# Window attention and two MLPs: an offset of its own for each group of operations in the planner's order

## The chip, the cores and the metric

One Trainium2 chip, one of its cores. The metric is the device time of one execution in microseconds (us); the kernel before took 952.38 us in the median of 3 runs (952.3 to 956.86).

Engines are named as the profile names them: PE (matrix products), PEld (its loads of weights), DVE, ACT, POOL (GpSimd) and SP (which issues the DMAs).

## What is computed

```python
def _attn_ref(q, k, v):                    # 4 batches, 8 heads, 576 positions, 64 wide
    scores = scale * np.matmul(q, k.transpose(0, 1, 3, 2))
    bias = slopes[:, None, None] * (-np.abs(rel))[None, :, :]
    mask = (rel >= 0) & (rel < 128)
    scores = np.where(mask, scores + bias[None], -1000000000.0)
    ...
    attn = attn / (np.sum(attn, axis=-1, keepdims=True) + 1e-09)
    return np.matmul(attn, v)

x = attention as 2304 tokens x 512
h = x @ w_in;   x = (h * tanh(softplus(h))) @ w_out      # moe:  512 -> 2048 -> 512
h = x @ w_in2;  out = elu(h) @ w_out2                    # moe2: 512 -> 2048 -> 512
```

## The kernel before, in words

**Work.** The tokens go in chunks of 512: chunk `ci` = 0 to 3 holds positions 0 to 511 of one batch, chunk 4 (`B`) the last 64 positions of all four. Attention is done by `unit(b, pr, part)`: one batch, one pair of heads, and queries 0 to 255 (`part` 0), 256 to 511 (1) or 512 to 575 (2). A unit is a chain over all engines: scores (PE, L493 to L503), masks and row minima (DVE, L514, L517), the exponential (ACT, L521), normalisation (L537 to L541: DVE, ACT or POOL), transposition (PE, L562), the mask again (L578 or L587), values (PE, L613), and a copy to SBUF.

**First MLP.** A step `s` of `hidden1` makes one 128x512 tile of hidden values: 12 products of 512 columns or 24 of 256, in pieces of six (L702), then on ACT the Mish function (L709, which needs another activation table than the exponential), a copy `gh` and a difference `gl` (L363) that together carry the value as high and low part. `output1` multiplies both with the second weights into `py` (L730), two steps later in the planner's count. Chunk 0 is done in 16 steps of half the width, so that its first half can start before all its attention is done; steps 16 to 71 are the other chunks. Every product is done three times (high by high, high by low, low by high).

**Weights.** The weights arrive as 64-bit numbers; `load_weights` turns each half of a 128-wide slice (32 for each MLP) into a high and a low part: two instructions on ACT, two on DVE, one on POOL, and then a copy and a difference on whichever engine is free. The 32 of the first MLP run beside attention at the start.

**Second MLP.** `hidden2` (L843), an ELU (L851 to L854, then `gh` and `gl`) and `output2` (L872), 80 steps. The hidden tile is in PSUM, in a ring of two buffers with the tag `h`: a third tile's products wait until the first one's `gl` has been taken.

**Order.** Nothing is emitted in the order of the source. Every operation is recorded in `Plan.op` with the engines that can do it (`ways`), its cost there, what it needs, its buffers and a priority `prio`. `Plan.order` then walks through time: each free engine takes the ready operation of lowest priority whose buffers have room, and where several engines could do it, the one that would finish first. The instructions of each engine stand in that order in the program, and each engine runs its own in order. So a priority decides both the order and the engine. Priorities are made of the step's planned time (`STEP` = 6.96) and offsets in the table `AT`, one for each kind of operation. While PE has nothing to do at the start, `order` puts products into its queue whose result nobody reads (`plan.fill`, L308, "unused"):

```python
if e == "pe" and self.fill and t < self.fill[2] and not self.rings["z"]["next"]:
    out.append(self.fill[1])
```

Of the kernel before, what the change touches and what calls it, by code (L numbers as in the profile page):

```python
# [13 lines left out]
AT = dict(lag=2, step=6.96, late=23.66, copy=1.19, both=0.34, conv=-34.61, conv1=8.2, mish=-3.26, out=-0.67,  # L14
          prep=-6.85, load=-27.75, loadr=12.24, unit=3.02, unit1=3.1, split=6.31, x2=-21.79, w2=1.86, step2=1.49,
          g=-8.44, stage=-21.52, fill=80.0, u0=0.0, u1=5.67, t0=1.26, t1=11.22, t2=4.45, u2=33.61, u3=4.87,
          norma=0.5, normp=8.33, relt=-13.66, d00=-2.11, d01=-2.85, d10=0.27, d11=1.21, dx=3.28, plain=6.14,
          mm2=8.39, first=-1000.0, second=-53.57, wadd=2.54, whi=-10.73, wlo=9.29, norm=-2.13, mask=-3.68, gl=13.52,
          newton=-9.59, elu=-24.7, lead=1, turn=2.71, held=28.54)
# [14 lines left out]
class Buffer:  # L34


    def __init__(self, ring, seq, make):
        self.ring, self.seq, self.make = ring, seq, make
        self.ops, self.real, self.left, self.taken, self.free_at = 0, None, 0, False, None
# [7 lines left out]
class Plan:  # L47
# [6 lines left out]

    WARM = 6.9
# [28 lines left out]
    def op(self, ways, reads=(), writes=(), prio=0.0, moved=0, rows=1.0, table=None, port=False):  # L84
# [20 lines left out]
        self.ops.append(dict(ways=ways, deps=deps, bufs=bufs, prio=prio, moved=moved, rows=rows, table=table, port=port))  # L105

    def order(self):
# [47 lines left out]
        while events:  # L155
# [4 lines left out]
            while again:  # L160
                again = False
                for e, q in waiting.items():
# [63 lines left out]
        return out  # L226

# [13 lines left out]
def mm_cost(n):  # L241
    return 0.000417 * n + 0.0125
# [18 lines left out]
def tile_window_attention_two_mlps(ctx, tc, qkv0, qkv1, qkv2, w1d, w2d, out):  # L261
    nc = tc.nc
# [45 lines left out]
    plan.fill = (256 / 2400 + 0.003, lambda: nc.tensor.matmul(unused[:, :256], ones[:, :P], ones[:, :256], start=True, stop=True), AT["fill"])  # L308
# [10 lines left out]
    def buf(tag, shape, dt=F32, name=None):  # L319
# [4 lines left out]
        def make():  # L324
            t = where.tile([P, words], dt, tag=tag, name=name or tag, bufs=slots)
# [8 lines left out]
        x = plan.buffer(tag, slots, make)  # L334
        return x

# [62 lines left out]
    def load_weights(wd, into, f, k, pr, stage):  # L399

        hi, lo = (buf(nm, (DM,), F32R) for nm in (("wih", "wil"), ("woh", "wol"))[k])
        into[f, k] = hi, lo
        for o in range(0, DM, HW):
# [24 lines left out]
                lambda hi=hi, o=o: hi()[:, o:o + HW], [bits] + [(hi, x) for x in parts], [(lo, x) for x in parts], pr + AT["wlo"])  # L428

# [3 lines left out]
    def unit(b, pr, part, t0, dt, banks, first=None):  # L433
# [8 lines left out]
        tp = t0 + AT["prep"] * dt  # L442
        cut = [sum(W[:i]) for i in range(4)]
# [21 lines left out]
        vn = lambda: vr().rearrange("p (n h d) -> p n h d", h=2, d=D)  # L465
        if not plain:
# [5 lines left out]
            sub(2 * nk, lambda: kk()[D:], lambda: k2()[D:], lambda: kk()[D:], [tiles[1]], [kk], tp)  # L472
        prob = []
# [176 lines left out]
        else:  # L650
            pieces = [(0, scores, 4), (3, turn, 4), (6, values, 0)]
        return [(t0 + o * dt, (lambda fn=fn, i=i, t=t0 + o * dt: fn(i, t))) for o, fn, i in pieces] + [
            (t0 + 8 * dt, lambda: finish(t0 + 8 * dt))]


    w1, w2, py_of, g_of = {}, {}, {}, {}
# [11 lines left out]
    def split_x(ci, t):  # L668
        need = [(b, 2) for b in range(B)] if ci == B else [(ci, 0), (ci, 1)]
# [3 lines left out]
        parts = range(n // C1)  # L673
        if ci == B:
# [29 lines left out]

# [247 lines left out]
```

## Time and profile before

| | |
|---|---|
| median of 3 runs | 952.38 us |
| the profiled execution | 954.04 us, its span 952.3 us (1.74 us lie around the span) |
| mean granted clock of PE | 0.983 of full speed |
| busy in the span | PE 932.0, PEld 775.9, DVE 514.6, ACT 505.8, POOL 175.1 us |

The span is one execution from the first instruction to the last. The clock that PE is granted has two levels, 1.2 and 2.4 GHz; a stretch's mean of 0.8 says that PE was at half speed in 40% of it. PE can lose time in two ways: it stands idle, or it works at half speed. Both are read from the view of stretches of time, which has the busy time of every engine and the granted clock of each stretch.

### The profile page before, as it was taken

Reading aid. Unit: us, or ns where it says so; the run is one execution under the profiler, and the core shown is the slowest. Engines: PE = TensorE matmul, PEld = TensorE weight load, DVE = VectorE, ACT = ScalarE, POOL = GpSimd, SP = SyncE. Lnnn points to the kernel's source line nnn. Section 1 sums busy time; section 2 is a strip of 40 time slices with the busy share of each in tenths; the row PEclk is TensorE's granted clock in tenths of the full one; section 3 lists DMA queues with packets and bytes.
Section 4 is the critical chain, followed back from the end, with each engine's and each line's share of the span. In section 5 each row is a group of like instructions: output and inputs, shape, how many; then the busy total and the mean of one; then the engine's idle time right before and its main releaser. Section 6 shows DMA issues by size and latency. Waiting matters only on the chain.

```text
span 952.3 us, 13731 instructions
## 1 busy us (share of the span) xinstructions
PE 932.0 (98%) x5061; PEld 775.9 (81%) x5061; DVE 514.6 (54%) x1305; ACT 505.8 (53%) x1022; POOL 175.1 (18%) x153
## 2 busy tenths in 40 slices
PE   9989998999999999999999999999999999999998
PEld 6668987978878777789988878888888888888887
DVE  7776878767623346871477796343334333333333
ACT  5788988785826566882477773233223222322232
POOL 2553454520100001010355552000000000000000
PEclk9789998999999999999999999999999999999999
DMA  8343445233212123440444541011001000100010
GB/s 237 118 134 114 158 156 179 91 121 107 77 35 70 42 59 103 131 138 34 124 157 141 166 154 34 1 45 45 1 0 41 27 1 1 44 1 1 1 45 23
DMA packets 32387, 75.08 MB, mean 79 GB/s; under 512 B 5696, under 2 KB 12352, under 8 KB 32320
## 3 DMA queue, kind: packets, MB, share of 16 engines
q1 hardware_dynamic: 32320, 74.20, 24.7%
q8 instruction: 40, 0.66, 0.3%
q14 instruction: 27, 0.22, 0.1%
HBM read 64.23 MB, written 9.96 MB: 78 GB/s over the span
## 4 chain that ended last, share of the span: by engine, by line
PE 79%; DVE 2%; ACT 1%; DMA 1%; issue 0%; DVEq 0%
PE py L872 21%; PE ph L843 20%; PE py L730 17%; PE ph L702 16%; PE ps_o L613 2%; PE ps_t L562 1%; PE ps_s L496 1%; PE ps_s L498 1%; PE ps_s L503 1%; DMA qkv<-in_qkv_dram 1%; DVE kk L363 0%; DMA x_scratch<-ys 0%; DVE ps_s L514 0%; DVE p L537 0%; DVE gl L363 0%
## 5 line engine op out<-in xcount | busy, mean ns | idle before, releaser
L363 DVE TENSOR_TENSOR gl<-ph,gh 128x512 fp32r<-128x512 f32 (+1 forms) x152 | 100.3, 660 | 168.7 <-ACT gh L353 168.2
L843 PE MATMUL ph<-x,wih 128*128 128x512 f32 (+1 forms) x640 | 181.8, 368 | 2.4 <-DVE gl L363 2.4
L353 ACT ACTIVATE gh<-ph 128x512 fp32r<-128x512 f32 (+1 forms) x143 | 81.6, 572 | 128.6 <-PE py L872 125.1
L843 PEld LDWEIGHTS ph<-x,wih 128*128 128x128 f32 x640 | 117.4, 188 | 25.4 <-DVE gl L363 3.1
L730 PE MATMUL py<-gh,woh 128*128 128x256 f32 (+1 forms) x384 | 136.2, 355 | 1.7 <-ACT gh L353 1.0
L702 PE MATMUL ph<-xh,wih 128*128 128x256 f32 (+1 forms) x384 | 134.5, 350 | 1.3 <-DVE gl L363 1.0
L730 PE MATMUL py<-gh,wol 128*128 128x256 f32 (+1 forms) x384 | 130.4, 340 | 1.0 <-DVE wol L363 0.6
L702 PE MATMUL ph<-xl,wih 128*128 128x256 f32 (+1 forms) x384 | 130.1, 339 | 0.7 <-DVE xl L363 0.7
L730 PE MATMUL py<-gl,woh 128*128 128x256 f32 (+1 forms) x384 | 130.3, 339 | 0.3 <-DVE gl L363 0.3
L702 PE MATMUL ph<-xh,wil 128*128 128x256 f32 (+1 forms) x384 | 130.0, 339 | 0.0
L843 PE MATMUL ph<-x,wil 128*128 128x512 f32 (+1 forms) x320 | 117.7, 368 | 0.0
L851 ACT ACTIVATE e<-ph 128x512 f32<-128x512 f32 (+1 forms) x80 | 44.4, 555 | 133.3 <-PE ph L843 132.4
L872 PE MATMUL py<-woh,gl 128*128 128x512 f32 x288 | 112.3, 390 | 0.0
L872 PE MATMUL py<-woh,gh 128*128 128x512 f32 x288 | 112.3, 390 | 0.0
L872 PE MATMUL py<-wol,gh 128*128 128x512 f32 x288 | 112.1, 389 | 0.0
L422 POOL TENSOR_TENSOR bits<-bits,raw 128x512 int32<-128x512 int32 x64 | 89.1, 1395 | 98.4 <-DVE bits L419 75.0
L852 DVE TENSOR_SCALAR e<-e 128x512 f32<-128x512 f32 (+1 forms) x80 | 34.7, 434 | 112.8 <-ACT e L851 112.5
L702 PEld LDWEIGHTS ph<-xh,wih 128*128 128x128 f32 x384 | 73.4, 191 | 13.0 <-issue 3.3
L730 PEld LDWEIGHTS py<-gh,woh 128*128 128x128 f32 x384 | 73.7, 192 | 10.9 <-issue 1.5
L730 PEld LDWEIGHTS py<-gh,wol 128*128 128x128 f32 x384 | 73.6, 192 | 9.6 <-DVE wol L363 1.0
L702 PEld LDWEIGHTS ph<-xh,wil 128*128 128x128 f32 x384 | 73.5, 192 | 7.8
L702 PEld LDWEIGHTS ph<-xl,wih 128*128 128x128 f32 x384 | 73.6, 192 | 7.6 <-DVE xl L363 0.9
(101 smaller groups left out, 1498.4 us busy)
## 6 DMA issues: line engine op xcount, KB each, us to landing
raw<-in_w_dram SPq DMA_DIRECT2D x64, 512.0 KB, 4.2
qkv<-in_qkv_dram SPq DMA_DIRECT2D x12, 640.0 KB, 4.0
qkv<-in_qkv_dram SPq DMA_DIRECT2D x16, 288.0 KB, 2.9
x_scratch<-ys SPq DMA_DIRECT2D x18, 256.0 KB, 2.2
out_dram<-yo SPq DMA_DIRECT2D x18, 256.0 KB, 2.0
qkv<-in_qkv_dram SPq DMA_DIRECT2D x8, 512.0 KB, 3.6
xr<-x_scratch SPq DMA_DIRECT2D x16, 256.0 KB, 2.8
v<-in_qkv_dram SPq DMA_DIRECT2D x12, 192.0 KB, 2.4
```

The costliest lines, as they stand in the source:

```text
L353: ways = [("act", act_cost(n, sbuf), lambda: nc.scalar.activation(o(), i(), AF.Copy), 0.0), ("dve", dve_cost(n, sbuf), lambda: nc.vector.t ...
L363: both(n, lambda eng: eng.tensor_tensor(out=o(), in0=i(), in1=hi().bitcast(F32), op=ALU.subtract), reads, writes, prio, only, port=not only)
L422: gps(HW, lambda raw=raw, bits=bits: nc.gpsimd.tensor_tensor(out=bits().bitcast(I32), in0=bits().bitcast(I32), in1=raw()[:, :, 0].bitcast( ...
L496: nc.tensor.matmul(o, qh()[:, j, qo:qo + r], kk()[:, j, ks], start=(j == 0), stop=False, skip_group_check=True)
L498: nc.tensor.matmul(o, ql()[:, j, qo:qo + r], kk()[:, j, ks], start=False, stop=True, skip_group_check=True)
L613: nc.tensor.matmul(o()[j * D:(j + 1) * D, c0:c0 + math.prod(y.shape[1:])], vn()[:kr, n, j], y, start=n == 0, stop=n == nkb - 1, skip_group ...
L702: nc.tensor.matmul(ph()[:, i * n:(i + 1) * n], wt()[:, cs], xx()[:, at], start=(c == 0 and m == 0), stop=(c == KC - 1 and m == 2))
L730: nc.tensor.matmul(py()[:, k, :], wt()[:, cs], gg()[:, i * n:(i + 1) * n], start=(f == 0 and a == 0 and k == 0), stop=(f == NF - 1 and a = ...
L843: nc.tensor.matmul(ph(), wt()[:, cs], xx(), start=(c == 0 and m == 0), stop=(c == KC - 1 and m == 2))
L851: act(n, lambda: nc.scalar.activation(e(), ph(), AF.Exp), [ph], [e], t, sbuf=False, table="exp")
L852: dve(n, lambda: nc.vector.tensor_scalar(out=e(), in0=e(), scalar1=1.0, scalar2=-1.0, op0=ALU.min, op1=ALU.add), (), [e], t, fast=True)
L872: nc.tensor.matmul(py(), gg()[:, ts_], wt(), start=(f == 0 and a == 0), stop=(f == NF - 1 and a == 2))
```

## The change

`Plan.op` adds an offset from a new table, `SHIFT`, to the priority of each operation of a named group. A group is one piece of a unit (`u1121`: batch 1, part 1, head pair 2, piece 1; `l`, `c`, `f` are its load, its copies, its end), one weight half (`w3_1` and `v3_1` for the first and second MLP), one gate (`g4`, `e4`: Mish or ELU of a step), or one step's products (`H4`, `O4`, `I4`, `P4`). 99 groups have an offset. Three numbers of `AT` change. `Plan.order` may put unused products in until 170 instead of 80, and `spare` is a new rule for more of them between others, which `ENOUGH` = 0 leaves without effect. `split_x` and `output1` are rewritten so that other widths of the steps could be chosen (`k0`, `k1`); with `k0` = 8 and `k1` = 0 they make the same operations as before. The same operations are in the program, apart from two unused products more and two loads of activation tables more.

```diff
-AT = dict(lag=2, step=6.96, late=23.66, ...
+AT = dict(lag=2, step=6.96, late=25.76, ...
...
-          g=-8.44, stage=-21.52, fill=80.0, u0=0.0, ...
-          norma=0.5, normp=8.33, relt=-13.66, ... wadd=2.54, ...
+          g=-8.44, stage=-21.52, fill=170.0, enough=0, u0=0.0, ...
+          norma=0.5, normp=8.33, relt=-15.35, ... wadd=1.47, ... k0=8, k1=0, u4=0.0, u5=5.67)
+
+SHIFT = dict(H10=139, H11=17.8, H15=98.9, H16=-42, H18=61.1, H22=14.7, H23=11.6, H3=-4.3, H5=-57.6, H6=2.9, H7=-3.9,
...
+             w15_0=-13, w15_1=10.1, w1_1=18.6, w7_0=-21, w7_1=59, w8_1=9.6, w9_0=41.3, z00=111.4, z01=-35.2)
@@ Plan.op
-        self.ops.append(dict(ways=ways, deps=deps, bufs=bufs, prio=prio, ...
+        prio += SHIFT.get(self.group, 0.0)
+        self.ops.append(dict(group=self.group, ways=ways, deps=deps, bufs=bufs, prio=prio, ...
@@ Plan.order
                     if best is None:
-                        if e == "pe" and self.fill and t < self.fill[2] and not self.rings["z"]["next"]:
+                        if e != "pe" or t > self.fill[2]:
+                            continue
+                        if t <= self.WARM or not self.rings["z"]["next"]:
                             out.append(self.fill[1])
-                            free[e] = self.clocked(t, self.fill[0], 1.0)
-                            heapq.heappush(events, free[e])
+                        else:
+                            b = self.spare(q, t)
+                            if b is None:
+                                continue
...
+    def spare(self, q, t):
+
+        k = int(t / self.TICK)
+        if self.columns.get(k, 0) + self.columns.get(k - 1, 0) * (k + 1 - t / self.TICK) > self.ENOUGH * self.COLUMNS:
+            return None
...
@@ hidden1 (output1, hidden2, output2, unit, load_weights, split_x: the same with their names)
+                plan.group = f"H{s}"
...
         gh, gl = buf("gh", (C2,), F32R), buf("gl", (C2,), F32R)
+        plan.group = f"g{s}"
```

The change reorders every engine's instructions. Counted over the whole program, operations that may run on several engines move too: ACT does 32 instead of 23 normalisations of `p` (DVE 112 instead of 121), 10 instead of 8 copies to `kk` of 128x768, and loads a table 73 instead of 71 times; POOL does seven operations fewer. In the first 25 us of the trace the order of PE is unchanged. Lines of the changed kernel are larger: L702 is L766 there, L730 L807, L843 L928, L562 L621, L613 L672, L493 L552, L496 L555, L498 L557, L709 L775, L521 L580, L539 L598, L414 and L417 L471 and L474, and the copies of L353 are at L406.

**First place.** ACT, around the first Mish (`ph<-ph`), that of step 0, beside the softmax of batch 0; `raw` and `wih` belong to weight halves. Before:

```order
57 L353 ACTIVATE wih<-bits 128x512
58 L521 ACTIVATE p,st<-p,st 128x128
59 L414 ACTIVATE raw<-raw 128x512
60 L521 ACTIVATE p,st<-p,st 128x128
61 L709 ACT_TABLE_LOAD
62 L709 ACTIVATE ph<-ph 128x512
63 L353 ACTIVATE xh_363<-ps_o 128x256
64 L539 ACTIVATE p<-p,st 128x128
65 L353 ACTIVATE pt<-ps_t 128x2x128
66 L521 ACT_TABLE_LOAD
```

After:

```order
47 L598 ACTIVATE p<-p,st 128x128
48 L580 ACTIVATE p,st<-p,st 128x128
49 L406 ACTIVATE xh_305<-ps_o 128x256
50 L775 ACT_TABLE_LOAD
51 L775 ACTIVATE ph<-ph 128x512
52 L598 ACTIVATE p<-p,st 128x128
53 L406 ACTIVATE pt<-ps_t 128x2x128 x2
54 L580 ACT_TABLE_LOAD
```

The Mish moved forward on ACT: 64 operations stand ahead of it, where it was 72.

**Second place.** PE, the transpositions `ps_t` of batch 1, part 1, third pair of heads, behind products of steps 10 and 11, and the scores `ps_s` of the fourth pair behind them. Before:

```order
809 L730 MATMUL py<-gh,woh 128x256
810 L730 MATMUL py<-gl,woh 128x256
811 L730 MATMUL py<-gh,wol 128x256
812 L562 MATMUL ps_t<-ident,p 128x128 x4
813 L496 MATMUL ps_s<-kk,q 128x256
814 L498 MATMUL ps_s<-kk,q 128x256
815 L496 MATMUL ps_s<-kk,q 128x256
816 L498 MATMUL ps_s<-kk,q 128x256
```

After:

```order
759 L621 MATMUL ps_t<-ident,p 128x128 x2
760 L766 MATMUL ph<-xh_426,wih 128x256
761 L766 MATMUL ph<-xl_433,wih 128x256
762 L766 MATMUL ph<-xh_426,wil 128x256
763 L766 MATMUL ph<-xh_487,wih 128x256
764 L766 MATMUL ph<-xl_492,wih 128x256
765 L766 MATMUL ph<-xh_487,wil 128x256
766 L621 MATMUL ps_t<-ident,p 128x128 x2
767 L555 MATMUL ps_s<-kk,q 128x256
768 L557 MATMUL ps_s<-kk,q 128x256
```

The pair's two transpositions stood together and are now parted by six products. Between this pair's scores and its first transposition there were 36 products of the MLP, now there are 42; between the fourth pair's scores and its transpositions (row 848 before, 856 after) there were 24, now 78.

**Third place.** PE, where the second MLP begins: `ph_5911` and `ph_5908` are its step 0, in two pieces of six products, and `py` the last step of the first MLP, in four pieces of three. Before, the first piece is followed by the four of `py`, then the second piece and step 1:

```order
2764 L843 MATMUL ph_5911<-x_5146,wih 128x512
2765 L843 MATMUL ph_5911<-x_5135,wil 128x512
2766 L730 MATMUL py<-gh,woh 128x512
2767 L730 MATMUL py<-gl,woh 128x512
...
2776 L730 MATMUL py<-gl,woh 128x512
2777 L730 MATMUL py<-gh,wol 128x512
2778 L843 MATMUL ph_5911<-x_5155,wih 128x512
2779 L843 MATMUL ph_5911<-x_5167,wih 128x512
```

After, both pieces stand ahead of them, and step 1 (`ph_5963`) follows:

```order
2767 L928 MATMUL ph_5908<-x_5148,wih 128x512
2768 L928 MATMUL ph_5908<-x_5137,wil 128x512
2769 L928 MATMUL ph_5908<-x_5157,wih 128x512
2770 L928 MATMUL ph_5908<-x_5169,wih 128x512
...
2774 L928 MATMUL ph_5908<-x_5183,wil 128x512
2775 L807 MATMUL py<-gh,woh 128x512
...
2786 L807 MATMUL py<-gh,wol 128x512
2787 L928 MATMUL ph_5963<-x_5127,wih 128x512
```

Step 0 of the second MLP is complete twelve products earlier, and its ELU has those twelve and the twelve of step 1 beside it, where it had the twelve of step 1.

## Rows read from the trace of the kernel before

**Rows 1.** The page, first part: busy time, share of the span and instructions of each engine.
```profile
PE 932.0 (98%) x5061; PEld 775.9 (81%) x5061; DVE 514.6 (54%) x1305; ACT 505.8 (53%) x1022; POOL 175.1 (18%) x153
```

**Rows 2.** The view of stretches; the whole span by stages; columns in its first line.
```profile
core 0: us, PE busy (x) PEld busy (x) DVE busy (x) ACT busy (x) POOL busy (x), PEclk, DMA share, GB/s
0.00:40.00 40.00, 38.04 (x197) 24.77 (x197) 28.84 (x144) 25.59 (x85) 12.57 (x27) 0.87 0.65 191
40.00:80.00 40.00, 34.59 (x219) 28.16 (x218) 32.13 (x89) 34.27 (x82) 22.38 (x25) 0.83 0.43 137
80.00:120.00 40.00, 39.81 (x319) 37.09 (x318) 30.70 (x80) 34.47 (x72) 16.85 (x12) 1.00 0.42 130
120.00:150.00 30.00, 26.84 (x218) 24.83 (x217) 23.75 (x60) 23.53 (x46) 12.91 (x10) 1.00 0.47 154
150.00:175.00 25.00, 22.35 (x163) 20.25 (x162) 22.97 (x51) 21.27 (x41) 13.56 (x10) 0.86 0.45 147
175.00:545.00 370.00, 369.25 (x2102) 306.06 (x2102) 213.51 (x612) 242.59 (x477) 72.80 (x54) 1.00 0.32 100
545.00:570.00 25.00, 22.64 (x100) 18.43 (x99) 21.87 (x27) 18.91 (x32) 15.18 (x12) 1.00 0.52 164
570.00:940.00 370.00, 370.00 (x1717) 309.38 (x1716) 138.16 (x242) 102.43 (x185) 8.88 (x8) 1.00 0.06 19
940.00:953.00 13.00, 8.47 (x44) 6.91 (x42) 2.71 (x7) 2.73 (x6) 0.00 (x0) 0.93 0.11 40
```

**Rows 3.** The view of waits, PE alone: us in total, times, longest.
```profile
PE ph L843 <- DVE gl L363: 2.4, 1, 2.4
PE ps_t L562 <- DVE p L537: 1.7, 2, 1.4
```

**Rows 4.** Instructions in order of time, 46 to 53 us: start, us, idle in brackets.
```profile
47.64 0.58 ACT L709 ACTIVATE ph<-ph 128x512 f32<-128x512 f32 x1
49.28 1.28 ACT L521 ACT_TABLE_LOAD   x1
50.57 0.40 ACT L521 ACTIVATE p<-p,st 128x128 f32<-128x128 f32 x1
51.55 0.68 DVE L363 TENSOR_TENSOR gl<-ph,gh 128x512 fp32r<-128x512 f32 x1
52.54 0.41 PE L730 MATMUL py<-gh,woh 128*128 128x256 f32 x1
```

**Rows 5.** The same view, 151 to 158 us: PE.
```profile
151.70 0.28 PE L730 MATMUL py<-gh,woh 128*128 128x256 f32 x1
151.82 0.28 PE L730 MATMUL py<-gl,woh 128*128 128x256 f32 x1
...
153.97 0.83 PE L562 MATMUL ps_t<-ident,p 128*128 128x128 f32 x4 [1.40 <-DVE p L537]
...
157.91 0.55 PE L702 MATMUL ph<-xh,wih 128*128 128x256 f32 x1 [0.50 <-DVE gl L363]
```

**Rows 6.** The view of stretches, 150 to 160 us; columns as in rows 2.
```profile
150.00:160.00 10.00, 7.35 (x46) 6.40 (x46) 9.82 (x28) 9.84 (x21) 4.96 (x4) 0.79 0.61 203
```

**Rows 7.** Instructions in order of time, 553 to 561 us: the second MLP's first steps.
```profile
554.94 0.61 PE L843 MATMUL ph<-x,wih 128*128 128x512 f32 x2
555.39 0.60 ACT L851 ACTIVATE e<-ph 128x512 f32<-128x512 f32 x1
557.43 0.39 PE L843 MATMUL ph<-x,wil 128*128 128x512 f32 x1
559.45 0.68 DVE L363 TENSOR_TENSOR gl<-ph,gh 128x512 fp32r<-128x512 f32 x1
560.18 0.73 PE L843 MATMUL ph<-x,wih 128*128 128x512 f32 x2 [2.36 <-DVE gl L363]
```

**Rows 8.** Groups of instructions, shapes apart, 0 to 175 us: count, busy us, mean ns.
```profile
L308 PE MATMUL unused<-const-bfloat16-1.0 128*128 128x256 bf16 x53 | 10.6, 358 | 0.8 <-PEq L938 0.8
L539 ACT ACTIVATE p<-p,st 128x128 f32<-128x128 f32 x17 | 5.9, 391 | 0.0
L353 ACT ACTIVATE kk<-qkv 128x768 fp32r<-128x768 f32 x4 | 3.3, 833 | 0.0
```

More of the change, by code (lines that the diff above doesn't have):

```diff
@@ L11 @@
 BF16 = mybir.dt.bfloat16
-AT = dict(lag=2, step=6.96, late=23.66, copy=1.19, both=0.34, conv=-34.61, conv1=8.2, mish=-3.26, out=-0.67,
+AT = dict(lag=2, step=6.96, late=25.76, copy=1.19, both=0.34, conv=-34.61, conv1=8.2, mish=-3.26, out=-0.67,
           prep=-6.85, load=-27.75, loadr=12.24, unit=3.02, unit1=3.1, split=6.31, x2=-21.79, w2=1.86, step2=1.49,
[L16 to L19, printed above, removed]
+          g=-8.44, stage=-21.52, fill=170.0, enough=0, u0=0.0, u1=5.67, t0=1.26, t1=11.22, t2=4.45, u2=33.61, u3=4.87,
+          norma=0.5, normp=8.33, relt=-15.35, d00=-2.11, d01=-2.85, d10=0.27, d11=1.21, dx=3.28, plain=6.14,
+          mm2=8.39, first=-1000.0, second=-53.57, wadd=1.47, whi=-10.73, wlo=9.29, norm=-2.13, mask=-3.68, gl=13.52,
+          newton=-9.59, elu=-24.7, lead=1, turn=2.71, held=28.54, k0=8, k1=0, u4=0.0, u5=5.67)
@@ L53 @@
     TICK, COLUMNS = 3.413, 3060
+    ENOUGH = AT["enough"]
     WARM = 6.9
@@ L226, in order @@
         return out
+    def spare(self, q, t):
+        k = int(t / self.TICK)
+        if self.columns.get(k, 0) + self.columns.get(k - 1, 0) * (k + 1 - t / self.TICK) > self.ENOUGH * self.COLUMNS:
+            return None
+        for i in sorted(q, key=lambda i: (self.ops[i]["prio"], i)):
+            bufs = self.ops[i]["bufs"]
+            if all(self.room(b, t) for b in bufs):
+                for b in bufs:
+                    if b.bank and (not b.taken or b.unused):
+                        b.unused = True
+                        return b
+        return None
     @staticmethod
@@ L324, in make @@
         def make():
-            t = where.tile([P, words], dt, tag=tag, name=name or tag, bufs=slots)
+            t = x.whole = where.tile([P, words], dt, tag=tag, name=name or tag, bufs=slots)
             n = math.prod(shape)
@@ L334, in buf, with grouped @@
         x = plan.buffer(tag, slots, make)
+        x.bank = where is psum
         return x
+    def grouped(name, fn, *a):
+        plan.group = name
+        fn(*a)
+        plan.group = None
     def act(n, emit, reads, writes, prio, sbuf=True, extra=0, table=None):
@@ L666, in operands, with split_x @@
         x_of[ci] = [(buf(f"xh{c}", (C2,), F32R), buf(f"xl{c}", (C2,), F32R)) for c in range(KC)]
-    def split_x(ci, t):
-        need = [(b, 2) for b in range(B)] if ci == B else [(ci, 0), (ci, 1)]
+    def split_x(ci, t, only=None):
+        need = [(b, 2) for b in range(B)] if ci == B else [(ci, x) for x in range(2) if only in (None, x)]
         if any((*x, pr) not in ended for x in need for pr in range(NPAIR)):
@@ L716, in output1 @@
         n = C2 // len(fs)
-        if fs[0] == 0:
-            py_of[ci, half] = [buf(tag, (C2 // n, n), name="py") for tag in ("yyzz" if n == C2 else "zz" if half else "yy")]
-        ys_of = py_of[ci, half]
+        if (ci, half) not in py_of:
+            if ci in (0, B):
+                py_of[ci, half] = [(buf("yz"[half], (2, C1), name="py"), half, (2 * y, 2 * y + 1)) for y in range(2)]
+            else:
+                py_of[ci, 0] = py_of[ci, 1] = [(buf(tag, (1, C2), name="py"), None, (y,)) for y, tag in enumerate("yyzz")]
@@ L720, in output1, with mm @@
         gh, gl = g_of.pop(s)
+        targets = py_of[ci, half] if n == C1 else [x for h in range(2) if ci == 0 or not h for x in py_of[ci, h]]
         for i, f in enumerate(fs):
             woh, wol = w1[f, 1]
[L723 to L728 removed]
+            for y, (py, only, cols) in enumerate(targets):
+                g0 = i * n if n == C1 else C1 * (only or 0)
+                o0 = half * C1 if only is None else 0
+                m = C1 if n == C1 or only is not None else C2
+                first = (ci, py) not in begun
+                begun.add((ci, py))
+                def mm(f=f, py=py, woh=woh, wol=wol, cols=cols, g0=g0, o0=o0, m=m, first=first):
+                    for k, c in enumerate(cols):
+                        cs = slice(c * P, (c + 1) * P)
```

97 lines of the change are left out of this document (68 added, 29 removed).

## Prediction

> **What bounds the kernel now.** I read the page's busy times first, then the view of stretches, PE's waits, and last the instructions in order of time where PE waits. The page says that PE is busy in 932.0 of 952.3 us [rows 1], so 20.3 us are idle. The stretches say where, and add what the granted clock costs [rows 2]: a stretch of 40 us at 0.83 has lost 0.17 x 40 = 6.8 us of full speed. By stage, idle plus clock: 0 to 40 us 2.0 + 5.2; 40 to 80 5.4 + 6.8; 80 to 120 0.2; 120 to 150 3.2; 150 to 175 2.7 + 3.5; 175 to 545 0.8; 545 to 570 2.4; 570 to 940 nothing; the end 3.8 + 0.9. That is 36.7 us in all. The kernel's time is PE's work, which the change leaves alone, plus this loss. So the question for each place is only how much of its loss goes, and what comes in its place.
>
> The clock follows the idle time. From 80 to 150 us it is 1.00; it is 0.83 in 40 to 80 and 0.86 in 150 to 175, the two stages in which PE waited much before. A wait that goes therefore takes some half speed with it, and a new one brings some.
>
> In none of these stages is another engine full on average: from 40 to 175 us (135 us) DVE is busy for 32.1 + 30.7 + 23.8 + 23.0 = 109.6 us and ACT for 34.3 + 34.5 + 23.5 + 21.3 = 113.5 [rows 2]. Each has a fifth of its time free while PE waits for it. What is missing is the order, with one exception: from 150 to 160 us DVE has 9.82 and ACT 9.84 of 10 us [rows 6]. There the work is too late, and only work done earlier helps.
>
> **The change, part by part.** *First 40 us.* PE's order is the same for the first 25 us, and the first two units of attention set the pace. Two more unused products stand there, of 0.36 us each [rows 8]: between 0 (they stand where PE waits) and 0.7; I take +0.4.
>
> *40 to 80 us, 12.2 us lost.* The first Mish starts at 47.64, its `gl` ends at 52.23, and PE's first product of `output1` follows at 52.54 [rows 4]. In the new order eight fewer operations stand ahead of this Mish on ACT; at about 0.4 us each (the normalisation's 0.391, rows 8) that is 3.2 us earlier. PE also has six more products ahead of that first use, 6 x 0.12 (the spacing of two neighbours, rows 5) = 0.7 us of cover. Ahead of the second `output1` step nothing of that kind changes, so its waits stay. Lower end: nothing, since the products put in between need the last attention of batch 0, which isn't earlier. Upper end: half the stage's loss, 6.1. I take 3, the 3.2 us of the Mish nearly whole, because that row is what ends the wait.
>
> *120 to 175 us, 9.4 us lost.* The largest wait is the transposition at 153.97, 1.40 us for DVE's `p`, and the clock is down until the products at 157.91 [rows 5]. The new order has 42 products instead of 36 between this pair's scores and its transposition, 0.7 us more, and six between its two transpositions, 0.7 us for the second. For the fourth pair it has 78 instead of 24: 6.5 us more. If each were enough, this pair's wait would shrink from 1.4 to 0.7, the fourth pair's would go, and with the idle time the 3.5 us of clock. Lower end: 0, if DVE and ACT stay full as in rows 6. Upper end: the 9.4. I take 5.5: all the clock (3.5) and 2 of the 5.8 us idle.
>
> *545 to 570 us, 2.4 us lost.* The ELU of step 0 needs 555.39 to 560.13 on ACT and DVE; PE ends step 1 (554.94 to 557.43, twelve products at 0.227) and waits 2.36 us for the ring [rows 3, 7]. From the end of step 0 at 554.94 to the end of `gl` it is 5.2 us. In the new order twelve more products of that size, 2.7 us, stand between: cover 5.4 instead of 2.7. So 5.4 against 5.2 leaves nothing of the wait, and 5.4 against 6.0, if the table load or DVE's queue adds 0.8, leaves 0.6. I take 1.8 back, ends 1.0 and 2.4. Step 71's own `gl` has less cover than before, 0.7 + 2.7 = 3.4 us instead of 4.1; its wait is in the rival on new waits.
>
> *More work on ACT.* Nine normalisations at 0.391, two copies at 0.833 and two table loads at 1.283: 3.5 + 1.7 + 2.6 = 7.8 us, most of it before 175 us [rows 4, 8]. Other copies come and go in equal number. Where ACT has room this costs nothing: 21.5 us are free between 40 and 175. Where it is full it delays PE. Together with waits at places that no row shows now I take +3; ends 0 and +7.8.
>
> A table load takes 1.28 us here, and the next instruction starts at its end: 49.28 + 1.28 = 50.56, then 50.57 [rows 4]. The Trainium skill (ScalarE: Activation LUTs, What ACT_TABLE_LOAD costs) says that each switch also costs a drain of about 1.38 us, 2.66 in all; no room for one is seen here. By that, the two loads would be 5.3 us and ACT's extra work 10.5.
>
> *The rest.* 80 to 120 and 175 to 940 have 3.3 us idle in all, of which 2.4 are counted above; nothing to gain. The end's order is the same: nothing.
>
> **Sum.** +0.4 - 3 - 5.5 - 1.8 + 3 = -6.9 us. The profiled execution took 954.04, which gives 947.1; it lies 1.66 us above the median of the runs, so as a median **945.5 us**. A measurement of this kernel tells 0.5% from no change, 4.8 us: faster is below 947.6, slower above 957.1.
>
> **Rivals.**
> *The waits move.* DVE and ACT limit the stage from 40 to 175 us, whatever the order, because both are four fifths busy and their work comes in chains; each wait that goes appears elsewhere. For it: 9.8 of 10 us in rows 6, and that ACT has more to do. Against it: the 15.7 us that ACT is free from 80 to 175 us. Only the beginning of the second MLP gains: 952.4 - 1.8 = 950.6.
>
> *ACT becomes the bound (slower).* Nearly all of the 7.8 us falls before the sixteenth step's Mish. From 80 to 175 us ACT is busy for 79.3 of 95 us; with 7.8 more it is 87.1, 92%. Once its share passes some 95%, the level of rows 6 where PE waits, each further microsecond reaches PE: the waits stay, 7.8 are added, 1.8 gained: 952.4 + 6.0 = 958.4. For it: the 9.84 of 10 us in rows 6. Against it: the free 15.7 us, if the work falls there.
>
> *Most of the waits go.* If the new offsets fit at all places, 40 to 80 gives 6.1, 120 to 175 all 9.4 and the second MLP 2.4: 17.9 us, with 3 back for new waits 14.9: 937.5. Against it: the start of this stage waits for attention itself, which has no cover yet.
>
> *It does nothing.* The rules for unused products (170, `spare`) yield only two more, so that part can't act; but the offsets do move every engine's order, as the three places show. No chance of its own.
>
> **Chances and range.** The forecast, a gain of 3 to 12 us: 0.50, of which 0.06 lies within 4.8 us. Most of the waits go: 0.13. The waits move: 0.25. ACT the bound: 0.12. So faster 0.44 + 0.13 = 0.57, same 0.06 + 0.25 = 0.31, slower 0.12. The range reaches from the third rival's 937.5 to beyond the second's 950.6 by the unpriced 3 us of new waits: 937.5 to 954.0; outside are the slower case and the better half of the third, under 0.2.
>
> **What would show it.** In the profile of the changed kernel: at 545 to 570 us an idle time under 1 us instead of 2.4 (right) or a new wait of the last step's `py` for `gl` (wrong). In the stretches the granted clock in 120 to 175 us at 1.00 and idle under 4 us; the transpositions of batch 1 with no wait over 1 us. First product of `output1` near 49 to 50 instead of 52.5 us. ACT's busy time about 8 us above 505.8. If the loss in 40 to 175 us is still near 21 us, the waits moved; if ACT is over 95% busy there and PE's waits name ACT, it is the bound. Wrong in another way: a loss above 2 us between 175 and 545 us, where PE has 0.8 us of idle time now, for example by attention that comes too late for the next chunk.

## The result, and the profile after

The changed kernel takes **944.13 us** in the median of 4 runs (939.99 to 947.3), the kernel before 952.68 in its 4 beside them; the ratio is 0.9898, with a 95% interval of 0.985 to 0.9945. So it is about 1% faster, 8.55 us, where 6.9 were forecast.

The page, first part, as in [rows 1]:

```profile
PE 924.7 (98%) x5063; PEld 771.5 (82%) x5063; DVE 510.8 (54%) x1301; ACT 509.9 (54%) x1035; POOL 168.5 (18%) x146
```

The stretches, with the columns of [rows 2]:

```profile
0.00:40.00 40.00, 36.27 (x194) 24.13 (x194) 27.67 (x144) 25.26 (x83) 13.51 (x28) 0.87 0.69 193
40.00:80.00 40.00, 36.38 (x243) 29.17 (x243) 33.61 (x102) 35.26 (x87) 24.50 (x25) 0.91 0.43 136
80.00:120.00 40.00, 39.47 (x323) 37.71 (x322) 31.16 (x74) 36.28 (x75) 14.10 (x10) 1.00 0.47 143
120.00:150.00 30.00, 25.14 (x209) 22.90 (x208) 25.67 (x71) 28.30 (x59) 12.20 (x9) 1.00 0.57 187
150.00:175.00 25.00, 24.24 (x196) 22.96 (x196) 23.77 (x42) 21.73 (x47) 15.40 (x11) 1.00 0.38 117
175.00:545.00 370.00, 369.76 (x2086) 305.82 (x2086) 212.10 (x602) 245.13 (x475) 71.06 (x53) 1.00 0.32 101
545.00:570.00 25.00, 25.00 (x111) 20.39 (x109) 23.46 (x35) 18.45 (x33) 13.11 (x10) 1.00 0.43 140
```

Read as before, idle plus clock: 0 to 40 us 3.7 + 5.2; 40 to 80 3.6 + 3.6; 80 to 120 0.5; 120 to 150 4.9; 150 to 175 0.8 and no clock; 175 to 545 0.2; 545 to 570 nothing. The stages no longer hold the same work, though: 4.9 us idle at 120 to 150 looks worse than 3.2, but the kernel is further on by then.

So the traces are also compared at **equal work**. For a moment t of the execution before, I count the columns of all matrix products that PE has started (unused ones left out), look up when the other execution has started as many, and subtract t. Negative is earlier. "early" offsets are those of groups that start before 80 us, "mid" before 180 us, "late" after 500 us; "numbers" are the three of `AT`; the last column is at 940 us.

```
t of before:                 40    80   120   165   175   545   570   940
changed kernel             +0.6  -2.0  -2.8  -7.7  -7.0  -7.2  -9.8 -10.0
e1 late offsets only       -3.8  -5.8  -5.8  -7.3  -7.4  -7.0  -9.5  -9.7
e2 numbers only            +0.5  +0.1  -0.8  -8.5  -7.3  -8.4  -8.5  -8.6
e3 numbers + early         -0.4  -0.5  +0.2  -2.5  -2.5  -2.5  -1.8  -1.7
e4 numbers + early + mid   +1.2  -1.5  -2.1  -5.5  -5.4  -6.6  -5.3  -5.4
e5 numbers + late          +0.6  +0.3  -0.6  -6.8  -6.9  -8.0 -10.5 -10.7
e6 late=27.86, no offset   +0.9  +0.9  +2.7  -0.2  +0.8  +1.4  +2.9  +2.8
e7 late=21.56, no offset   -0.2  +1.8  +0.6  -0.4  +0.3  +5.4  +6.2  +6.2
e8 changed, more on ACT    -1.0  -2.6  -3.7  -6.8  -6.8  -7.2  -9.7  -9.8
e9 before, no addition     -0.1  -5.1  -5.2  -6.1  -6.2  -6.0  -6.1  -6.2
e10 numbers, no addition   -4.7  -6.5  -7.0 -14.7 -14.8 -15.8 -16.0 -16.1
e11 changed, 29 unused     +3.6  +0.5  -0.8  -3.1  -3.0  -3.3  -5.8  -6.0
e12 changed, 70 unused     +0.4  +7.9  +6.5  +3.8  +4.3 +12.5 +10.0  +9.8
```

Each row is one execution, and executions of one order differ too. The changed kernel, e4 (up to 174 us), e8 and e11 have the same order on PE, apart from unused products, and gain 4.9, 3.4, 3.1 and 2.3 us from 120 to 165. At 80 us e1 stands at -5.8 and e2 at +0.1, though PE and ACT have the order of the kernel before in both up to 71 us. So a step of 2 us in one row is not yet the order's; what the medians say counts more.

In this pair of executions the changed kernel gains at three places: 2 us before 80, 4.2 between 120 and 175 and 2.6 at the beginning of the second MLP. The first is not shown to come from the order: e3, which has the changed kernel's order up to 75 us, gains 0.5 by 80, and e1, in the old order, 5.8. At the second MLP the ELU has ended before PE wants its ring again (timeline of the changed kernel; start, us):

```profile
545.62 0.61 ACT L938 ACTIVATE e<-ph 128x512 f32<-128x512 f32 x1
547.27 0.39 PE L807 MATMUL py<-gh,wol 128*128 128x512 f32 x1
549.86 0.68 DVE L416 TENSOR_TENSOR gl<-ph,gh 128x512 fp32r<-128x512 f32 x1
551.86 0.62 PE L928 MATMUL ph<-x,wih 128*128 128x512 f32 x2
```

`gl` ends at 550.54, step 1 and the first `output2` products keep PE busy until 551.86, and the 2.36 us in brackets of [rows 7] are gone.

Between 120 and 175 us what moved is attention. The last products of values of each of the four pairs of heads of batch 1, part 1, in the kernel before:

```profile
127.25 1.09 PE L613 MATMUL ps_o<-pt,v 128*64 128x128 f32 x12
147.18 1.09 PE L613 MATMUL ps_o<-pt,v 128*64 128x128 f32 x12
159.46 1.98 PE L613 MATMUL ps_o<-pt,v 128*64 128x128 f32 x12
166.14 1.09 PE L613 MATMUL ps_o<-pt,v 128*64 128x128 f32 x12
```

and in the changed kernel:

```profile
122.70 1.09 PE L672 MATMUL ps_o<-pt,v 128*64 128x128 f32 x12
134.38 1.09 PE L672 MATMUL ps_o<-pt,v 128*64 128x128 f32 x12 [1.10 <-issue]
148.10 1.09 PE L672 MATMUL ps_o<-pt,v 128*64 128x128 f32 x12
160.53 1.09 PE L672 MATMUL ps_o<-pt,v 128*64 128x128 f32 x12
```

The second pair's values followed the first's after 19.9 us; now it is 11.7. Before, two pairs' work fell together at 150 to 160 us, where DVE and ACT were full [rows 6]; now it is spread. ACT is as full there as it was, but PE is busy for 9.69 us instead of 7.35 (view of stretches, the changed kernel), so a full ACT by itself was not what PE waited for:

```profile
150.00:160.00 10.00, 9.69 (x80) 9.39 (x80) 8.90 (x17) 9.85 (x22) 4.48 (x4) 1.00 0.54 177
```

### The profile page after: what moved, and what is told of

It reads as the page before. It is cut to its first block, busy times and chain, and to the rows that moved or that the text cites. A ratio compares the mean times of both kernels' runs of the same rounds, so it can differ in the third digit from the quotient of the medians.

```text
span 942.3 us, 13722 instructions
## 1 busy us (share of the span) xinstructions
PE 924.7 (98%) x5063; PEld 771.5 (82%) x5063; DVE 510.8 (54%) x1301; ACT 509.9 (54%) x1035; POOL 168.5 (18%) x146
## 4 chain that ended last, share of the span: by engine, by line
PE 87%; DVE 5%; ACT 4%; DMA 1%; SPq 1%; issue 1%; POOL 0%; ACTq 0%
PE ph L928 21%; PE py L960 21%; PE py L807 19%; PE ph L766 18%; PE ps_o L672 3%; DMA raw<-in_w_dram 1%; PE ps_t L621 1%; DVE bits L473 1%; SPq L503 1%; PE ps_s L555 1%; PE ps_s L557 1%; PE ps_s L552 1%; ACT p L580 1%; ACT raw L471 1%; PE ps_s L562 1%
## 5 line engine op out<-in xcount | busy, mean ns | idle before, releaser
L928 PE MATMUL ph<-x,wih 128*128 128x512 f32 (+1 forms) x640 | 181.6, 367 | 0.0
L406 ACT ACTIVATE gh<-ph 128x512 fp32r<-128x512 f32 (+1 forms) x140 | 79.9, 573 | 128.8 <-PE py L960 122.2
L766 PE MATMUL ph<-xh,wih 128*128 128x256 f32 (+1 forms) x384 | 135.0, 352 | 2.0 <-DVE gl L416 1.8
L928 PEld LDWEIGHTS ph<-x,wih 128*128 128x128 f32 x640 | 117.7, 188 | 22.4
L807 PE MATMUL py<-gh,woh 128*128 128x256 f32 (+1 forms) x384 | 134.1, 349 | 0.2 <-ACT gh L406 0.2
L807 PE MATMUL py<-gl,woh 128*128 128x256 f32 (+1 forms) x384 | 129.7, 338 | 0.9 <-DVE gl L416 0.9
L766 PE MATMUL ph<-xl,wih 128*128 128x256 f32 (+1 forms) x384 | 129.7, 338 | 0.4 <-DVE xl L416 0.4
L766 PE MATMUL ph<-xh,wil 128*128 128x256 f32 (+1 forms) x384 | 129.6, 338 | 0.3 <-DVE wil L416 0.3
L807 PE MATMUL py<-gh,wol 128*128 128x256 f32 (+1 forms) x384 | 129.6, 337 | 0.2 <-DVE wol L416 0.2
L928 PE MATMUL ph<-x,wil 128*128 128x512 f32 (+1 forms) x320 | 117.6, 368 | 0.0
L766 PEld LDWEIGHTS ph<-xh,wih 128*128 128x128 f32 x384 | 73.3, 191 | 13.6 <-issue 4.5
L807 PEld LDWEIGHTS py<-gh,woh 128*128 128x128 f32 x384 | 72.8, 190 | 8.8 <-issue 1.4
L766 PEld LDWEIGHTS ph<-xh,wil 128*128 128x128 f32 x384 | 73.1, 190 | 8.3 <-DVE wil L416 0.5
L807 PEld LDWEIGHTS py<-gh,wol 128*128 128x128 f32 x384 | 72.8, 190 | 8.4 <-DVE wol L416 0.4
L766 PEld LDWEIGHTS ph<-xl,wih 128*128 128x128 f32 x384 | 73.2, 191 | 7.3 <-DVE xl L416 0.6
```

What stands on the lines that cost most here:

```text
L406: ways = [("act", act_cost(n, sbuf), lambda: nc.scalar.activation(o(), i(), AF.Copy), 0.0), ("dve", dve_cost(n, sbuf), lambda: nc.vector.t ...
L766: nc.tensor.matmul(ph()[:, i * n:(i + 1) * n], wt()[:, cs], xx()[:, at], start=(c == 0 and m == 0), stop=(c == KC - 1 and m == 2))
L807: nc.tensor.matmul(py()[:, k, o0:o0 + m], wt()[:, cs], gg()[:, g0:g0 + m], start=(first and a == 0 and k == 0), stop=(f == NF - 1 and a == 2),
L928: nc.tensor.matmul(ph(), wt()[:, cs], xx(), start=(c == 0 and m == 0), stop=(c == KC - 1 and m == 2))
```

## The experiments

**Which part of the table gains? (e1 to e4)** All four are the changed kernel with part of its table:

```diff
 e1:  three numbers of AT as before
-SHIFT = dict(H10=139, ...)          # 99 groups
+SHIFT = dict(I2=-48.2, I6=16.9, O70=-46.7, P0=-94, P13=0.5, P29=-9.4, P4=11.4, e0=-3.5, e1=-4, v11_1=-33.9, v13_1=28.1)
 e2:  new numbers
+SHIFT = dict()
 e3:  new numbers, the 23 offsets of groups that start before 80 us
 e4:  new numbers, the 63 offsets of groups that start before 180 us
```

> The old table and only those 11 of the new offsets that act around the beginning of the second MLP (its steps 0 to 29 and the last weights). Places add up (mine): the order is the old one up to 540 us, so the loss up to there is as before; the 2.4 us idle in 545 to 570 go, and nothing else: 950 us, ratio 0.9975. Waits move (rival): the idle time in 545 to 570 comes back within 30 us, as a wait for gl of the first MLP's last step or of the next ELU: 952 to 953, ratio 1.000.

Measured: 949.89 (944.31 to 950.98), ratio 0.9964 (0.9942 to 0.9985), 3 us less than the 952.94 before. At equal work its profiled execution, the fastest of its 11, gains 2.5 us at the second MLP and nothing else that the program explains: the 5.8 us before 80 us stand in a part of the order that is that of before, and come from the clock (below). This place is separate, and the 11 late offsets are what brings it.

> The three changed numbers of the old table (late, relt, wadd) and none of the new offsets. Places add up (mine): the offsets make the gain, so this stays within 2 us of before, 950 to 954, with a loss of 18 to 24 us in 40 to 175 us. Rival: the second halves of the weights, 2.1 later in the order, make the gain of the first 300 us; then 945 to 946 and a loss of 14 us or less in 40 to 175.

Measured: 944.5 (939.86 to 951.17), ratio 0.9909 (0.9882 to 0.9937): the three numbers, without one offset, gain as much as the whole change. My range is missed, the rival's nearly met. It is one number: with `late` alone at 25.76 every engine's order is the same as with all three. `late` is the planned distance between the two halves of a weight slice in `load_weights`; the second halves, for `output1`, are planned 2.1 us later. At equal work the gain is there at once between 120 and 165 us, from -0.8 to -8.5, and the pairs of attention have moved as in the changed kernel:

```profile
123.02 1.09 PE L662 MATMUL ps_o<-pt,v 128*64 128x128 f32 x12
135.04 1.09 PE L662 MATMUL ps_o<-pt,v 128*64 128x128 f32 x12
148.68 1.09 PE L662 MATMUL ps_o<-pt,v 128*64 128x128 f32 x12
157.52 1.09 PE L662 MATMUL ps_o<-pt,v 128*64 128x128 f32 x12
```

Here too the second pair is 12.0 us behind the first, and the third and fourth follow at 13.6 and 8.8. ACT in the stretch from 120 to 150 us, the kernel before and this one (ACT's busy time is the fourth, after DVE's):

```profile
120.00:150.00 30.00, 26.84 (x218) 24.83 (x217) 23.75 (x60) 23.53 (x46) 12.91 (x10) 1.00 0.47 154
```

```profile
120.00:150.00 30.00, 27.86 (x232) 25.75 (x232) 26.01 (x75) 29.04 (x59) 16.51 (x13) 1.00 0.58 194
```

> The three numbers and the offsets of groups that begin before 80 us alone. Places add up (mine): the loss in 40 to 80 us falls from 12.2 to some 7, as in the changed kernel, that of 120 to 175 us stays near 9: 947 to 949 us. Waits move (rival): what is won before 80 us is lost by 175 us, because DVE and ACT limit that stage: 951 to 953.

Measured: 951.69 (947.29 to 954.78), ratio 0.9977 (0.996 to 0.9995). That is the rival's range, but not for its reason: little is won before 80 us (-0.5) that could be lost by 175, and from 120 to 165 the row gains 2.7 us.

> The three numbers and the offsets of groups that begin before 180 us. Places add up (mine): loss in 40 to 175 us as in the changed kernel (14 us), the 2.4 us at 545 to 570 stay: 946 to 947 us; the offsets of 180 to 240 us then bring nothing, since PE had 0.8 us of idle time there. Rival: those later offsets carry part of the gain (attention put off past 240 us): 948 to 950, with idle time over 1.5 us between 175 and 545.

Measured: 948.6 (947.4 to 949.05), ratio 0.9953 (0.9922 to 0.9983). The time is in the rival's range, but PE is idle for 0.1 us from 175 to 545, not for over 1.5. The early offsets (e3) take back most of what the number gave: at 120 us they are no further than before (+0.2, e2 -0.8), and from 120 to 165 they gain 2.7 us where the number alone gains 7.7. The mid offsets restore a part in the median (948.6 instead of 951.69). So the offsets before 500 us are another way to about the same time, not an addition to what the number brings.

**Is the number alone better? (e5 to e7)**

```diff
 e5:  new numbers, the 11 late offsets only
 e6:  no offset, late=27.86
 e7:  no offset, late=21.56
```

> The new three numbers and only the 11 late offsets (the products, gates and weight halves that start after 500 us); no offset of attention, of the first MLP or of its weight halves. Theory (the places add up, and the one number `late` brings what is gained before 175 us): 944.5 of the run with the three numbers alone, less the 2.4 us of the second MLP's first wait, is 942.1; idle at 545 to 570 us under 0.5 us, the loss from 40 to 175 us 9 to 15 us. Rival (the early offsets are needed as well, and the run with the three numbers alone was lucky with the clock): 946 to 949, slower than the changed kernel's 944.1.

Measured: 943.29 (938.05 to 946.85), ratio 0.9881 (0.9846 to 0.9916) to 953.14 before. At equal work the places add up: to e2's gain e5 adds 2.5 us at the second MLP (-8.0 to -10.5). The medians differ by 1.2, less than the spread of either (942.1 was expected). One number and 11 offsets give the time of three numbers and 99 (944.13); the runs cannot tell the two apart.

> The kernel with no offset at all, and `late`, the planned distance between the two halves of a weight slice, at 27.86: moved from the old 23.66 by 4.2 instead of 2.1. Theory (the second halves stand in the way of attention and of the first MLP, so later is better until the second product must wait for them): 940 to 945, at most half a microsecond more than 944.5, with PE waits that name `woh` or `wol` if it is too far. Rival (any new number draws one order out of many that differ by several us, without a direction): anywhere from 944 to 956, as likely above 949 as below.

Measured: 958.21 (953.28 to 962.94), ratio 1.0042 (1.0016 to 1.0067), slower than before.

> The same kernel with `late` at 21.56, moved by 2.1 the other way. Theory (later is better): slower than before by about what the new number gained, 957 to 962, with more idle time of PE between 40 and 175 us. Rival (a draw without a direction): 944 to 956, as likely faster than before as slower.

Measured: 960.19 (954.9 to 968.86), ratio 1.0073 (1.0045 to 1.0102), slower too. Four values of one number, 2.1 apart, give 960, 953, 944.5 and 958. "Later is better" fits e7 and fails for e6, and the sign that it named for "too far" is missing: PE's waits for `woh` and `wol` come to 0.7 us in e6, to 1.7 in the kernel before. The rival's range misses both times. That the number has no direction is the likelier reading, but four values do not show it. In this reading a priority picks one order out of many; what it means in the plan says little about which.

**Is ACT the bound now? (e8)** A copy that nothing reads, on ACT, in each weight half of the first MLP:

```diff
-            act(HW, lambda raw=raw: nc.scalar.activation(raw()[:, :, 0] ... scale=2.0 ** -29), ...
+            act(HW, lambda raw=raw: (nc.scalar.activation(raw()[:, :, 0] ... scale=2.0 ** -29),
+                [nc.scalar.activation(spare_act, ident[:, :8], AF.Copy) for _ in range(1 * (wd is w1d))]), ...
```

> The changed kernel with one more copy of 128x8 on ACT in each of the 32 weight halves of the first MLP, which nothing reads: by the line through the 128x128 operation's 0.39 us and the 128x768 copy's 0.83 us some 0.3 us each, 10 us in all, most of it between 15 and 175 us. Theory (ACT is not the bound; it is free for 13 us of 135 between 40 and 175 us): 944 to 948. Rival (ACT is the bound there, as it is busy for 9.85 of 10 us from 150 to 160): each added microsecond reaches PE, 951 to 954, with more PE waits that end on ACT or on what DVE does behind it.

Measured: 945.71 (944.21 to 945.98), ratio 0.9909 (0.9881 to 0.9936). The added work is smaller than expected (groups of instructions, busy us and mean ns):

```profile
L474 ACT ACTIVATE spare_act<-ident 128x8 f32<-128x8 f32 x32 | 6.6, 207 | 0.0
```

Of 6.6 us, 1.6 appear in the median, within the spread. At equal work the rows end 0.2 us apart, but e8 was 1.6 us ahead at 40 us, where its granted clock was 0.91 instead of 0.87, and has lost that by 175. So at most a quarter of the added work reaches PE, and the rival's "each added microsecond" is excluded, though ACT is busy for 28.6 of 30 us at 120 to 150.

**Does ACT stand behind POOL? (e9, e10)** In the kernel before ACT is idle for 6.5 us from 120 to 150; its longest wait there is a copy to `wih` that waits 1.9 us for POOL's `bits`. The same orders without that POOL operation:

```diff
-            gps(HW, lambda raw=raw, bits=bits: nc.gpsimd.tensor_tensor(
+            gps(HW, lambda raw=raw, bits=bits: None if wd is w1d else nc.gpsimd.tensor_tensor(
```

> The kernel before, with PE's, ACT's and DVE's order unchanged, but without POOL's addition (`bits<-bits,raw`, 1.3 us each) in the 32 weight halves of the first MLP; those weights then lack their last bits. Theory (before, ACT stands in its order behind weight halves that wait for POOL, 2.7 us of its 6.5 us idle from 120 to 150 us, and the work left over piles up at 150 to 160, where PE then waits): the same products are reached 4 to 8 us earlier at 165 us, ACT is busy for 26 us or more of the 30 from 120 to 150 instead of 23.5, and the time is 944 to 949. Rival (attention's own chain of DVE and ACT sets the pace there, the weight halves only fill ACT's free time): 951 to 953, less than 2 us earlier at 165 us.

Measured: 948.32 (944.06 to 957.16), ratio 0.9953 (0.9914 to 0.9991). The time is in the theory's range, but not for its reason: at equal work the gain stands before 80 us (-5.1), where e1 has as much with nothing left out; from 120 to 165 it is 0.9 us, and ACT is busy for 24.6 of the 30 us from 120 to 150, not for 26. The pairs keep their spacing of 19.4 us between the first and the second:

```profile
121.45 1.09 PE L662 MATMUL ps_o<-pt,v 128*64 128x128 f32 x12
140.82 1.09 PE L662 MATMUL ps_o<-pt,v 128*64 128x128 f32 x12
```

> The kernel with the new number alone (no offsets), in the same way without POOL's addition in the first MLP's weight halves. Theory (its order no longer has ACT behind POOL there: 0.5 us of such waits from 120 to 150 us): at most 2 us less than its 944.5, 942 to 945. Rival (the weight halves' chains are long at every place, and shorter chains help whatever the order is): as much is gained as in the run on the kernel before, 936 to 940.

Measured: 939.11 (935.92 to 944.79), ratio 0.9874 (0.9827 to 0.9922): 5.4 us less than with the addition, about as much as on the kernel before (4.0). The rival holds, and this theory of mine falls. Without the addition 0.9 us is gained at 120 to 165 with the old order and 0.0 more with the new one (7.7 in both): the gain there comes with the order, not with the addition.

**What the number moves.** A likely cause stands in the queue of loads. In the kernel before SP issues the load of the third pair's `qkv` at 135.94, 20 us after the second pair's at 115.90 (instructions in order of time, SP's queue):

```profile
115.90 0.33 SPq L446 DMA_DIRECT2D qkv<-in_qkv_dram  x1
117.88 9.57 SPq L409 DMA_DIRECT2D raw<-in_w_dram  x4
128.38 0.33 SPq L446 DMA_DIRECT2D v<-in_qkv_dram  x1
135.94 0.33 SPq L446 DMA_DIRECT2D qkv<-in_qkv_dram  x1
```

Of this it waits 7.2 us for POOL's `bits` (view of waits, SP, 110 to 150 us; the longest is the last number):

```profile
SPq L446 <- POOL bits L422: 9.6, 2, 7.2
```

That is a weight half: `RAW` stages every fifth half of the first MLP in the only `qkv` buffer, and its users take turns in the order in which they are recorded, which follows their planned time. With `late` at 23.66 a weight half has its turn between the second pair and the third; with 25.76 it comes behind the third. In PE's order the second pair's values stand behind the third pair's scores, which need this load, so both pairs are late, and the third falls together with the fourth. PE does not wait at these scores, though: `kk` is ready at 143.90, and PE comes to them at 144.48 with no idle time before (instructions in order of time, the kernel before):

```profile
142.48 1.42 DVE L363 TENSOR_TENSOR kk<-qkv,kk 64x768 fp32r<-64x768 f32 x1 [0.86 <-ACT kk L353]
144.48 0.28 PE L496 MATMUL ps_s<-kk,q 128*128 128x256 f32 x1
```

So the turn acts through the plan, which reckons with it and puts the scores that late, and not as a wait for the load. The pair's first wait is its transposition's 1.40 us at 153.97 [rows 5]. In e2 the load is issued 6.7 us after the second pair's:

```profile
111.66 0.33 SPq L493 DMA_DIRECT2D qkv<-in_qkv_dram  x1
112.92 0.33 SPq L453 DMA_DIRECT2D raw<-in_w_dram  x1
118.35 0.33 SPq L493 DMA_DIRECT2D qkv<-in_qkv_dram  x1
```

The changed kernel has the same turn (111.28 and 119.63). All runs fall into two groups by it: with the old turn (e1, e7, e9) 0.9 to 1.5 us are gained at equal work from 120 to 165 us, with the new one 2.3 (e11) to 7.7 (e2, e10). e9's load still comes 17.9 us after the one before it (109.25, 127.10), since the half in the buffer has its other steps to go through. e3, e6 and e12 have the new turn as well and end at 951.69, 958.21 and 963.03, so it is no warrant of a good order. The old turn is seen in two orders only, that of the kernel before (with e1 and e9) and that of e7.

The cover that the prediction counted is a rival to the turn, and goes with the gain too. Between scores and transposition of the third and of the fourth pair there stand 36 and 24 products of the first MLP in the kernel before, 54 and 30 in e7, 42 and 78 in the changed kernel, and 84 and 60 in e2, e5 and e10, which gain most; but e12 has 12 and 36 and gains 2.7 us. The turn was read from the traces and the program; a kernel that changes it and nothing else was not tried, so which of the two makes the gain is not shown.

**The unused products (e11, e12)**

```diff
 e11: only the first 29 of 55 are emitted, the order else unchanged
+    products = itertools.count()
-    plan.fill = (..., lambda: unused_product(unused), AT["fill"], unused_before)
+    plan.fill = (..., lambda: unused_product(unused) if next(products) < 29 else None, AT["fill"], unused_before)
 e12:
-          ... fill=170.0, enough=0, ...
+          ... fill=170.0, enough=1.0, ...
```

> The changed kernel with the first 29 of its 55 unused products; the other 26, which stand where PE waits between 20 and 40 us, are left out. Theory (they stand in waits, so they cost nothing, and they keep the granted clock up): without them PE works longer at half speed between 20 and 60 us, 945 to 949. Rival (the waits there are set by attention's chain on DVE and ACT, which half speed of PE does not lengthen): 943 to 945.

Measured: 946.97 (945.24 to 949.17), ratio 0.9944 (0.9916 to 0.9972), 2.8 us above the changed kernel; the two spreads overlap (its highest time is 947.3). Of the 26 products left out only ten start after 20 us, from 26.1 to 28.4; the others start from 7.9 to 18.9. The first 40 us:

```profile
0.00:40.00 40.00, 37.40 (x145) 24.13 (x146) 24.39 (x130) 22.71 (x79) 11.45 (x26) 0.66 0.69 191
```

The granted clock is 0.66 instead of 0.87, a loss of 13.6 us instead of 5.2; only 3.0 of these 8.4 are seen at equal work at 40 us. The time is in the theory's range, and the products seem to earn their place; but most of this clock loss lies beside attention's chain, as the rival said.

> The changed kernel with ENOUGH = 1.0 instead of 0, so that the new rule puts further unused products into PE's waits until 170 us: 70 in all instead of 55. Theory (the clock still costs 5.2 + 3.6 us from 0 to 80 us, and products in the waits raise it): clock loss from 40 to 175 us under 2 us, 939 to 943. Rival (each unused product stands in PE's order and delays what is behind it when the wait is shorter than planned, 15 of 0.36 us or less): 944 to 949.

Measured: 963.03 (961.72 to 964.56), ratio 1.0115 (1.0076 to 1.0154). The rival holds in sign, and its 5 us are far too few: the 15 products take 3.1 us of PE, but the planner counts them, and everything behind them is ordered anew. At equal work 7.5 us are lost from 40 to 80 us, where the 15 stand. PE loses another 8 us between 175 and 300 us, where there are none of them, and ACT waits for POOL at 120 to 150 us as it did before:

```profile
ACT wih L406 <- POOL bits L476: 2.1, 2, 1.8
```

So the run doesn't tell what the products cost by themselves; it tells that the rule, switched on with this table, is worse by 19 us.

## Why the prediction was right, step by step

At equal work the measured steps stand beside the terms of the sum: first 40 us +0.6 (forecast +0.4); 40 to 80 -2.6 (-3); 120 to 175 -4.2 (-5.5); 545 to 570 -2.6 (-1.8); the rest -1.2 (0). These come to -10.0 where the four terms gave -9.9; they are steps of one pair of executions. **The step that failed is the +3 for ACT's extra work and new waits.** ACT's busy time rose by 4.1 us instead of 7.8: the other copies did not come and go in equal number, they fell by 3.7. And e8 shows that of 6.6 us more on ACT at most 1.6 reach PE. New waits came, but at these places, and are in their numbers. The medians differ by 8.55, which leaves 1.4 at most for this term; the forecast said 6.9, and 944.13 is well within 937.5 to 954.0.

*40 to 80 us: near in size by luck, wrong in its reason.* The first Mish starts 4.5 us earlier (43.10 instead of 47.64) and its `gl` ends at 50.81 instead of 52.23, yet the first product of `output1` is later, 53.81 instead of 52.54, not at 49 to 50:

```profile
43.10 0.58 ACT L775 ACTIVATE ph<-ph 128x512 f32<-128x512 f32 x1
50.12 0.69 DVE L416 TENSOR_TENSOR gl<-ph,gh 128x512 fp32r<-128x512 f32 x1
53.81 0.28 PE L807 MATMUL py<-gh,woh 128*128 128x256 f32 x1
```

At 60 us nothing is gained (0.0). The row that I took for the end of a wait had no wait before it: PE was at half speed there, and arrived late enough by itself [rows 4]. What shrinks is the waits of the second `output1` step, where I had seen nothing. In the kernel before and in the changed one they are

```profile
67.09 1.54 PE L493 MATMUL ps_s<-qkv 64*128 64x128 f32 x8 [0.84 <-DMA qkv<-in_qkv_dram]
69.65 0.38 PE L730 MATMUL py<-gh,woh 128*128 128x256 f32 x1 [1.01 <-ACT gh L353]
```

```profile
66.21 1.54 PE L552 MATMUL ps_s<-qkv 64*128 64x128 f32 x8 [0.18 <-DMA qkv<-in_qkv_dram]
67.97 0.38 PE L807 MATMUL py<-gh,woh 128*128 128x256 f32 x1 [0.21 <-ACT gh L406]
```

These shorter waits come with the order: e1, in the old one, has 0.84 and 1.02 us again, e4, in the new one, 0.17 and 0.23. In this execution the clock of 60 to 80 us also goes from 0.91 to 1.00. But the size of the step is not the order's: from 40 to 80 us e3, in the changed kernel's order up to 75 us, gains 0.1 us, e8 1.6 and e11 3.1, while e1, in the old order, gains 2.0.

*120 to 175 us: right place, nearly the size.* The transposition's 1.40 us wait [rows 5] and the 3.5 us of clock went. That the clock follows the idle time, which put the 3.5 into the term, is no rule here: 545 to 570 us had 2.4 us idle at 1.00 before, and 120 to 150 us have 4.9 idle at 1.00 in the changed kernel. Nor was full speed back at 157.91: the third pair's values at 159.46 took 1.98 us instead of 1.09. The reason is half shown: I counted products that stand between scores and transposition as cover. What goes with the gain in all runs is that the third pair's load comes 7 to 11 us after the second's instead of 18 to 20, and in most of them the cover is larger too; the two were not parted. The rows of a full DVE and ACT [rows 6] said "only work done earlier helps"; I should have followed that work back to its load, in SP's queue.

*545 to 570 us.* Right; the whole 2.4 went, for the cover that the order showed, and e1 and e5, with the 11 late offsets, confirm it.

*The rivals.* "The waits move" would have given 950.6: they moved within 120 to 150 (4.9 us idle instead of 3.2), but not the sum. "ACT becomes the bound" is excluded by the time and by e8. Of the signs, the clock of 120 to 175 us came out (1.00), its idle time did not (5.6 us, not under 4); the loss from 40 to 175 is 13.4 us, not 21. What the prediction had no eye for is that 88 of the 99 offsets aren't needed.

## What to carry to other kernels

Compare executions of a reordered program at equal work, not stage by stage: the stages no longer hold the same products, and a stage's idle time can rise while the kernel gains. Take more than one execution of each order before a step of 2 us is given a reason. An offset in a greedy planner is a draw among orders; offsets of separate places add up (second MLP), those of one place undo each other, so try one number at a time and keep what the times on the chip say. Where two engines are full for 10 us, follow their work back to its load: a buffer that two kinds of work share can set an order that no engine's busy time shows.

## What was not expected of the hardware

One program's executions differ by more than the 8.55 us of the change, and the granted clock goes with it: e2's eight spread over 11 us, its shortest span 938.1 us with a mean granted clock of 0.996, its longest 949.5 with 0.983. The same early order ran once at 1.00 for the first 40 us (e1) and once at 0.87 [rows 2]:

```profile
0.00:40.00 40.00, 36.22 (x210) 24.59 (x211) 33.10 (x163) 29.10 (x100) 15.38 (x31) 1.00 0.69 198
```

which was worth 3.8 us at 40 us. But a slower clock costs less where PE would wait anyhow. At 48 to 54 us e2 has the order of the kernel before; from 48 to 52 us that one ran at 1.2 GHz (0.50) and had no wait at the first product of `output1` [rows 4], while e2 ran at 2.4 GHz (1.00) and waited twice:

```profile
50.24 0.38 PE L797 MATMUL py<-gh,woh 128*128 128x256 f32 x1 [0.44 <-DVE gh L397]
51.38 0.39 PE L797 MATMUL py<-gl,woh 128*128 128x256 f32 x1 [0.76 <-DVE gl L406]
```

From 40 to 60 us the clock of the two differs by 5.2 us (0.74 against 1.00), but e2 gains only 1.9 at equal work. So here idle time and clock loss of one stretch, which the prediction added, were not two separate gains.
